# Loading a K cache in 8 KB rows and scoring four heads at once, in an attention decode kernel

## Chip, cores, metric

One core of a Trainium2 chip. The metric is device time in microseconds (us), lower is better. A program on one core has no other cores to be compared with, so a run counts as fast unless it is over 1.5% above the fastest of the same kernel; single looks have the state "unknown".

## The reference

```python
B, Sq, D = 32, 1, 512
Hq, Hkv, Sk, Dh = 32, 8, 2048, 128
W = 512                                   # the last 512 keys count
q = (x @ wq).reshape(B, 1, Hq, Dh)        # 4 query heads share one K/V head
k = k_cache[:, :, Sk - W:, :]             # per batch and head: 512 rows of 256 bytes, contiguous
v = v_cache[:, :, Sk - W:, :]
p = softmax(q @ k^T * Dh ** -0.5)
out = (p @ v) @ wo
```

All data is bf16. Of each batch the kernel reads 1 MB of K and 1 MB of V (8 heads x 512 keys x 256 bytes), for 32 batches; with wq and wo (4 MB each) that is 75.5 MB. Nothing is read twice. The window of one head is 128 KB long, and the next head's window begins 512 KB further on.

## The kernel before

SyncE (SP) issues all loads in one queue: K and V of each batch in turn, K into 4 slots, V into 12. For each batch TensorE transposes K in 32 pieces of 128 x 128 into PSUM (the memory that its results go to), VectorE copies three quarters of it back and ScalarE one quarter, and TensorE makes the scores: eight matmuls, one for each K/V head, of 32 weights columns and 512 moving columns. The weights (QBD) are zero except for the four query heads that belong to that K/V head, so eight accumulating matmuls fill 32 rows. Softmax, the transpose of P and the product with V are done for four batches (a quad) at a time.

```python
def load_k(b):                                    # on SP
    if b >= NK:
        sp.wait_ge(pe_T3, b - NK + 1)             # slot free: transposes of batch b-4 done
    sp.dma_start(
        K_sb[:, b % NK, :, :],
        k_cache[b, :, SK - W:, :].rearrange("g (p kt) d -> p g (kt d)", kt=KT),
    ).then_inc(sem_k[b % NK], 16)
# ...
for g in range(G):                                # scores, on TensorE
    # ... wait for the eviction of head g
    last = pe.matmul(
        S_ps[32 * j:32 * (j + 1), q % 2, :],      # j: batch in its quad
        lhsT=QBD[:, b % NQB, g, :],
        rhs=KT_sb[:, b % NKT, g, :],
        start=(g == 0), stop=(g == G - 1), tile_position=(0, 32 * j),
    )
```

The access pattern of the K load: partition p takes keys 4p to 4p+3 of each head, in memory 128 rows at an even pitch, each with 8 pieces (the heads) of 1 KB.

## Time and profile before

229.98 us, median of 3 runs (229.43 to 230.52). The page of the profile, cut; rows of digits are 40 equal slices of the span, 9 is busy to 90% or more:

```profile
span 228.2 us, 5628 instructions
PE 176.6 (77%) x2501; PEld 124.7 (55%) x2501; DVE 90.0 (39%) x237; ACT 48.1 (21%) x93; POOL 9.4 (4%) x43
...
DMA  6999999999999999999999999999999999999950
GB/s 188 386 385 348 348 348 349 348 348 350 349 347 348 349 347 348 348 348 348 348 348 348 347 348 348 348 348 348 347 347 348 347 348 347 349 345 329 350 183 6
DMA packets 72950, 75.90 MB, mean 333 GB/s; under 512 B 1184, under 2 KB 70880, under 8 KB 72928
...
DMA 53%; PE 26%; SPq 16%; issue 2%; DVEq 0%; DVE 0%; ACT 0%
...
L234 PE MATMUL KT_ps<-ident,K_sb 128*128 128x128 bf16 x1024 | 74.3, 240 | 29.7 <-DMA K_sb<-in_k_cache_dram 25.6
L254 PE MATMUL S_ps<-KT_sb,QBD 128*32 128x512 bf16 x256 | 68.2, 414 | 2.8 <-POOL QBD L191 2.8
...
K_sb<-in_k_cache_dram SPq DMA_DIRECT2D x32, 1024.0 KB, 12.1
V_sb<-in_v_cache_dram SPq DMA_DIRECT2D x24, 1024.0 KB, 12.0
```

The DMA row is full from the second slice until the last loads, and the rate stays near 348 GB/s while K and V are loaded; TensorE is busy 77% of the time and VectorE 39%. The loads bound the kernel. The second and third slices hold wq alone, and run at 386: wq comes in packets of 2 KB, K, V and wo in packets of 1 KB.

The same by stretches (columns: stretch and length in us, busy time and instructions of each engine, granted TensorE clock, DMA share, GB/s):

```profile
core 0: us, PE busy (x) PEld busy (x) DVE busy (x) ACT busy (x) POOL busy (x), PEclk, DMA share, GB/s
26.00:60.00 34.00, 26.35 (x350) 18.38 (x347) 13.84 (x39) 7.78 (x15) 1.05 (x5) 0.95 1.10 349
...
170.00:194.00 24.00, 21.81 (x289) 15.77 (x289) 9.17 (x26) 4.53 (x9) 0.00 (x0) 0.79 1.10 348
```

The rate is the same where TensorE's clock was 0.95 and where it was 0.79: compute does not set the pace.

### The profile page before, as it was taken

To read this page: it belongs to the slowest core of one execution; us is meant where nothing else is said; L and a number is where in the kernel's file an instruction comes from. 1 tells how busy PE (TensorE), PEld (TensorE's weight loads), DVE (VectorE), ACT (ScalarE), POOL (GpSimd) and SP (SyncE) were. 2 spreads that over 40 slices of the span, in tenths; PEclk is the share of its full clock that TensorE was granted. 3 is DMA by queue.
4 is the path that set the end of the run, shared out by engine and by line. 5 is a ranking of instruction groups with operands and counts; after the bars stand their busy time and mean duration, and the time that the engine had idled before them with its cause. 6 is when DMAs were issued, how large, how long until landed. Compare 5 with 4: busy or idle time off the path is not lost.

```text
span 228.2 us, 5628 instructions
## 1 busy us (share of the span) xinstructions
PE 176.6 (77%) x2501; PEld 124.7 (55%) x2501; DVE 90.0 (39%) x237; ACT 48.1 (21%) x93; POOL 9.4 (4%) x43
## 2 busy tenths in 40 slices
PE   0184968669869986995997996699669799999482
PEld 0182555447635753575564964477437656695340
DVE  0047333351535243633275243524353317644212
ACT  2000103122113211320133021321132013403203
POOL 5002000000000000000000000000000000000000
PEclk9998879999997999797699889889997859979855
DMA  6999999999999999999999999999999999999950
GB/s 188 386 385 348 348 348 349 348 348 350 349 347 348 349 347 348 348 348 348 348 348 348 347 348 348 348 348 348 347 347 348 347 348 347 349 345 329 350 183 6
DMA packets 72950, 75.90 MB, mean 333 GB/s; under 512 B 1184, under 2 KB 70880, under 8 KB 72928
## 3 DMA queue, kind: packets, MB, share of 16 engines
q1 hardware_dynamic: 72928, 75.57, 103.7%
q8 instruction: 19, 0.31, 0.6%
q14 instruction: 3, 0.02, 0.0%
HBM read 75.53 MB, written 0.03 MB: 331 GB/s over the span
## 4 chain that ended last, share of the span: by engine, by line
DMA 53%; PE 26%; SPq 16%; issue 2%; DVEq 0%; DVE 0%; ACT 0%
DMA K_sb<-in_k_cache_dram 48%; PE KT_ps L234 12%; PE S_ps L254 7%; PE QO_ps L286 6%; SPq L142 6%; DMA wo_sb<-in_wo_dram 5%; SPq L132 5%; SPq L149 4%; SPq L124 2%; PE PT_ps L266 1%; PE KT_ps L315 0%; DVEq L43 0%; DVE X_sb L389 0%; PE QO_ps L324 0%; ACT out_sb L441 0%
## 5 line engine op out<-in xcount | busy, mean ns | idle before, releaser
L234 PE MATMUL KT_ps<-ident,K_sb 128*128 128x128 bf16 x1024 | 74.3, 240 | 29.7 <-DMA K_sb<-in_k_cache_dram 25.6
L348 DVE COPY KT_sb<-KT_ps 128x512 bf16<-128x512 bf16 x192 | 68.0, 418 | 68.0 <-PE KT_ps L234 67.3
L234 PEld LDWEIGHTS KT_ps<-ident,K_sb 128*128 128x128 bf16 x1024 | 67.8, 108 | 42.1 <-DMA K_sb<-in_k_cache_dram 34.9
L254 PE MATMUL S_ps<-KT_sb,QBD 128*32 128x512 bf16 x256 | 68.2, 414 | 2.8 <-POOL QBD L191 2.8
L405 ACT ACTIVATE KT_sb<-KT_ps 128x512 bf16<-128x512 bf16 x64 | 34.7, 594 | 161.6 <-PE KT_ps L234 161.6
L254 PEld LDWEIGHTS S_ps<-KT_sb,QBD 128*32 128x32 bf16 x256 | 23.7, 102 | 34.8 <-issue 8.2
L286 PEld LDWEIGHTS QO_ps<-PT_sb,V_sb 128*128 128x128 bf16 x768 | 20.0, 97 | 3.2 <-ACT PT_sb L422 2.1
L286 PE MATMUL QO_ps<-PT_sb,V_sb 128*128 128x4 bf16 x768 | 20.7, 165 | 0.8 <-ACT PT_sb L422 0.7
L370 DVE CAST oT_sb<-QO_ps 128x128 bf16<-128x128 f32 x8 | 5.8, 719 | 38.8 <-PE QO_ps L286 38.8
L191 POOL COPY QBD<-QT_sb 128x32 bf16<-128x32 bf16 x32 | 6.3, 209 | 152.7 <-PE S_ps L254 135.8
L214 PE MATMUL QO_ps<-xT_sb,big_sb 128*128 128x32 bf16 x128 | 4.1, 185 | 8.4 <-DMA big_sb<-in_wq_dram 8.3
L336 DVE CAST QT_sb<-QO_ps 128x512 bf16<-128x512 f32 x2 | 4.8, 2393 | 13.0 <-PE QO_ps L214 13.0
L214 PEld LDWEIGHTS QO_ps<-xT_sb,big_sb 128*128 128x128 bf16 x128 | 3.8, 103 | 8.7 <-issue 6.7
L286 PEld LDWEIGHTS QO_ps<-PT_sb,big_sb 128*128 128x128 bf16 x256 | 6.5, 96 | 0.8 <-ACT PT_sb L422 0.8
L286 PE MATMUL QO_ps<-PT_sb,big_sb 128*128 128x4 bf16 x256 | 6.7, 164 | 0.0
L413 ACT ACTIVATE P_f_56<-S_ps,negmax 128x512 f32<-128x512 f32 x8 | 5.5, 687 | 4.0 <-DVE negmax L356 4.0
L354 DVE TENSOR_REDUCE maxv<-S_ps 128x1 f32<-128x512 f32 x8 | 5.5, 682 | 1.0 <-PE S_ps L254 1.0
L266 PE MATMUL PT_ps<-ident,P_bf 128*128 128x128 bf16 x32 | 3.6, 242 | 2.5 <-DVE P_bf L364 2.5
L422 ACT ACTIVATE PT_sb<-PT_ps 128x512 bf16<-128x512 bf16 x8 | 4.8, 604 | 1.2 <-PE PT_ps L266 1.2
L315 PE MATMUL KT_ps<-wo_sb,oT_sb 128*32 128x512 bf16 x32 | 3.9, 626 | 0.9 <-DVE oT_sb L370 0.8
L266 PEld LDWEIGHTS PT_ps<-ident,P_bf 128*128 128x128 bf16 x32 | 2.5, 111 | 3.0 <-DVE P_bf L364 3.0
L364 DVE TENSOR_SCALAR P_bf<-P_f_56,recip 128x512 bf16<-128x512 f32 x8 | 3.9, 486 | 0.3
(25 smaller groups left out, 14.7 us busy)
## 6 DMA issues: line engine op xcount, KB each, us to landing
K_sb<-in_k_cache_dram SPq DMA_DIRECT2D x32, 1024.0 KB, 12.1
V_sb<-in_v_cache_dram SPq DMA_DIRECT2D x24, 1024.0 KB, 12.0
big_sb<-in_v_cache_dram SPq DMA_DIRECT2D x8, 1024.0 KB, 12.0
big_sb<-in_wq_dram SPq DMA_DIRECT2D x4, 1024.0 KB, 10.8
wo_sb<-in_wo_dram SPq DMA_DIRECT2D x4, 1024.0 KB, 12.0
x_sb<-in_x_dram SPq DMA_DIRECT2D x1, 32.0 KB, 1.6
out_dram<-out_sb SPq DMA_DIRECT2D x1, 32.0 KB, 1.5
```

The costliest lines, as they stand in the source:

```text
L132: sp.dma_start(K_sb[:, b % NK, :, :], k_cache[b, :, SK - W:, :].rearrange("g (p kt) d -> p g (kt d)", kt=KT),).then_inc(sem_k[b % NK], 16)
L142: sp.dma_start(v_slot(b)[:, :, :], v_cache[b, :, SK - W:, :].rearrange("g (p kt) d -> p g (kt d)", kt=KT),).then_inc(sem_v[b % NV], 16)
L149: sp.dma_start(wo_sb[:, c * 8:(c + 1) * 8, :], wo[c * 1024:(c + 1) * 1024, :].rearrange("(h d) n -> d h n", d=P),).then_inc(sem_wo[c], 16)
L191: pool.tensor_copy(dst, src).then_inc(pool_qbd, 1)
L214: last = pe.matmul(QO_ps[:, hl * 32:(hl + 1) * 32], lhsT=wq_sb[:, kt, h * DH:(h + 1) * DH], rhs=xT_sb[:, kt, :], start=(kt == 0), stop=(kt ...
L234: last = pe.matmul(KT_ps[:, t, half * 512 + kt * 128: half * 512 + (kt + 1) * 128], lhsT=K_sb[:, b % NK, g, kt * DH:(kt + 1) * DH], rhs=id ...
L254: last = pe.matmul(S_ps[32 * j:32 * (j + 1), q % 2, :], lhsT=QBD[:, b % NQB, g, :], rhs=KT_sb[:, b % NKT, g, :], start=(g == 0), stop=(g = ...
L266: last = pe.matmul(PT_ps[:, kt * 128:(kt + 1) * 128], lhsT=P_bf[:, qq % 2, kt * 128:(kt + 1) * 128], rhs=ident[:, :], start=True, stop=Tru ...
L286: last = pe.matmul(QO_ps[:, j * 32 + 4 * g: j * 32 + 4 * g + 4], lhsT=v_slot(b)[:, g, kt * DH:(kt + 1) * DH], rhs=PT_sb[:, qq % 2, kt * 12 ...
L348: dve.tensor_copy(KT_sb[:, b % NKT, g, :], KT_ps[:, t, half * 512:(half + 1) * 512]).then_inc(dve_T, 1)
L370: dve.tensor_copy(oT_sb[:, :, 4 * qq:4 * qq + 4].rearrange("p h j -> p j h"), QO_ps[:, 0:128].rearrange("p (j h) -> p j h", h=HQ),).then_i ...
L405: act.activation(KT_sb[:, b % NKT, g, :], KT_ps[:, t, half * 512:(half + 1) * 512], ACTF.Copy).then_inc(act_T, 1)
```

## The change

Its intent: read K in rows of 8 KB, so that there are 128 large packets per batch instead of 1024 small ones, and let four score matmuls run at once on four column groups of TensorE's array (32 columns each, by `tile_position`). Partition p = 8 s + g now holds 32 keys in a row (the s-th of 16 groups) of head g. Transposing such a tile through a permutation matrix, not the identity, brings the keys of a head side by side. Score matmuls of heads g and g + 4 accumulate in the rows of column group g % 4; scores are made one batch later, and pairs of evictions become one. P is read in permuted order to match V.

```diff
-                    K_sb[:, b % NK, :, :],
-                    k_cache[b, :, SK - W:, :].rearrange("g (p kt) d -> p g (kt d)", kt=KT),
+                    K_sb[:, b % NK, :],
+                    k_cache[b, :, SK - W:, :].rearrange("g (s r) d -> s g (r d)", s=16),
 ...
+            pool.affine_select(
+                out=perm[:, :, :], in_=perm[:, :, :], compare_op=ALU.not_equal, fill=1.0,
+                base=0, pattern=[[-1, G], [-8, 16]], channel_multiplier=1,
 ...
+                    for i in range(8):
+                        r = 8 * t + i
+                        last = pe.matmul(
+                            KT_ps[:, t, i * 128:(i + 1) * 128],
+                            lhsT=K_sb[:, b % NK, r * DH:(r + 1) * DH],
+                            rhs=perm[:, :, :],
 ...
-                        S_ps[32 * j:32 * (j + 1), q % 2, :],
+                        S_ps[32 * (g % 4):32 * (g % 4) + 32, q % 2, :],
                         lhsT=QBD[:, b % NQB, g, :],
-                        rhs=KT_sb[:, b % NKT, g, :],
-                        start=(g == 0), stop=(g == G - 1), tile_position=(0, 32 * j),
+                        rhs=KT_sb[:, b % NKT, :, g, :],
+                        start=(j == 0 and g < 4), stop=(j == 3 and g >= 4), tile_position=(0, 32 * (g % 4)),
 ...
-                    for half in range(2):
-                        g = 2 * t + half
-                        dve.tensor_copy(
-                            KT_sb[:, b % NKT, g, :], KT_ps[:, t, half * 512:(half + 1) * 512]
-                        ).then_inc(dve_T, 1)
+                    dve.tensor_copy(
+                        KT_sb[:, b % NKT, 8 * t:8 * t + 8, :, :], KT_ps[:, t, :]
+                    ).then_inc(dve_T, 1)
 ...
-                    P_bf[:, qq % 2, :], P_f32[:, qq % 2, :], recip[:, qq:qq + 1], None, op0=ALU.mult
+                    P_bf[:, qq % 2, :].rearrange("p (kt s u) -> p kt s u", kt=KT, s=16),
+                    P_f32[:, qq % 2, :].rearrange("p (u kt s) -> p kt s u", kt=KT, s=16),
+                    recip[:, qq:qq + 1], None, op0=ALU.mult,
```

The K load of the changed kernel reads 16 groups (8 KB apart) of 8 rows (512 KB apart) of 4096 elements and writes 128 partitions; before it read 128 groups of 8 pieces of 512 elements.

More of the change, by code (lines that the diff above doesn't have):

```diff
@@ L47, in bass_standalone__sliding_block_cached__sampling_kernel @@
         wo_sb = es.enter_context(nc.sbuf_tensor([P, HQ, D], BF16))
-        K_sb = es.enter_context(nc.sbuf_tensor([P, NK, G, KT * DH], BF16))
+        K_sb = es.enter_context(nc.sbuf_tensor([P, NK, 32 * DH], BF16))
         V_sb = es.enter_context(nc.sbuf_tensor([P, NVA, G, KT * DH], BF16))
-        KT_sb = es.enter_context(nc.sbuf_tensor([P, NKT, G, W], BF16))
+        KT_sb = es.enter_context(nc.sbuf_tensor([P, NKT, 32, G, 16], BF16))
         QT_sb = es.enter_context(nc.sbuf_tensor([P, B, HQ], BF16))
@@ L58, in bass_standalone__sliding_block_cached__sampling_kernel @@
         ident = es.enter_context(nc.sbuf_tensor([P, P], BF16))
+        perm = es.enter_context(nc.sbuf_tensor([P, G, 16], BF16))
         X_sb = es.enter_context(nc.sbuf_tensor([P, D], BF16))
@@ L91, in bass_standalone__sliding_block_cached__sampling_kernel @@
         pool_R = es.enter_context(nc.semaphore("pool_R"))
+        pool_perm = es.enter_context(nc.semaphore("pool_perm"))
         dve_xT = es.enter_context(nc.semaphore("dve_xT"))
@@ L113, in v_slot, with prow @@
             return Vx_sb[:, s - NVA]
+        def prow(g, j):
+            return 32 * (g % 4) + 16 * (g // 4) + 4 * j
         def quad_of(b):
@@ L172, in _ @@
             ).then_inc(pool_init, 1)
+            pool.memset(perm[:, :, :], 0.0).then_inc(pool_perm, 1)
+            pool.wait_ge(pool_perm, 1)
+            pool.affine_select(
+                out=perm[:, :, :], in_=perm[:, :, :], compare_op=ALU.not_equal, fill=1.0,
+                base=0, pattern=[[-1, G], [-8, 16]], channel_multiplier=1,
+            ).then_inc(pool_perm, 1)
             pool.memset(QBD[:, :, :, :], 0.0).then_inc(pool_init, 1)
@@ L188, in _ @@
                 n = b % NQB
-                dst = bass.AP(tensor=QBD, offset=n * G * 32, ap=[[qbd_row, P], [36, G], [1, REP]])
-                src = bass.AP(tensor=QT_sb, offset=b * HQ, ap=[[qt_row, P], [REP, G], [1, REP]])
+                dst = bass.AP(
+                    tensor=QBD, offset=n * G * 32 + 4 * (b % 4),
+                    ap=[[qbd_row, P], [144, 2], [32, 4], [1, REP]],
+                )
+                src = bass.AP(
+                    tensor=QT_sb, offset=b * HQ, ap=[[qt_row, P], [4 * REP, 2], [REP, 4], [1, REP]]
+                )
                 pool.tensor_copy(dst, src).then_inc(pool_qbd, 1)
@@ L222, in transposes @@
             def transposes(b):
+                if b == 0:
+                    pe.wait_ge(pool_perm, 2)
                 pe.wait_ge(sem_k[b % NK], 16 * (b // NK + 1))
@@ L226, in transposes @@
                         if t < 3:
-                            pe.wait_ge(dve_T, 6 * (b - 1) + 2 * (t + 1))
+                            pe.wait_ge(dve_T, 3 * (b - 1) + t + 1)
                         else:
-                            pe.wait_ge(act_T, 2 * b)
+                            pe.wait_ge(act_T, b)
                     last = None
-                    for half in range(2):
-                        g = 2 * t + half
-                        for kt in range(KT):
-                            last = pe.matmul(
-                                KT_ps[:, t, half * 512 + kt * 128: half * 512 + (kt + 1) * 128],
-                                lhsT=K_sb[:, b % NK, g, kt * DH:(kt + 1) * DH],
-                                rhs=ident[:, :],
-                                start=True, stop=True, is_transpose=True, tile_position=(0, 0),
-                            )
+                    for i in range(8):
[4 more added lines that the diff above has]
+                            rhs=perm[:, :, :],
+                            start=True, stop=True, is_transpose=True, tile_position=(0, 0),
+                        )
                     last.then_inc(pe_T[t], 1)
@@ L248, in s_matmuls @@
                 last = None
+                pe.wait_ge(dve_T, 3 * b + 3)
+                pe.wait_ge(act_T, b + 1)
                 for g in range(G):
-                    if g < 6:
-                        pe.wait_ge(dve_T, 6 * b + g + 1)
-                    else:
-                        pe.wait_ge(act_T, 2 * b + (g - 6) + 1)
                     last = pe.matmul(
-                        S_ps[32 * j:32 * (j + 1), q % 2, :],
+                        S_ps[32 * (g % 4):32 * (g % 4) + 32, q % 2, :],
                         lhsT=QBD[:, b % NQB, g, :],
-                        rhs=KT_sb[:, b % NKT, g, :],
-                        start=(g == 0), stop=(g == G - 1), tile_position=(0, 32 * j),
+                        rhs=KT_sb[:, b % NKT, :, g, :],
+                        start=(j == 0 and g < 4), stop=(j == 3 and g >= 4), tile_position=(0, 32 * (g % 4)),
                     )
@@ L288, in pv_matmuls @@
                                 lhsT=v_slot(b)[:, g, kt * DH:(kt + 1) * DH],
-                                rhs=PT_sb[:, qq % 2, kt * 128 + j * 32 + 4 * g: kt * 128 + j * 32 + 4 * g + 4],
+                                rhs=PT_sb[:, qq % 2, kt * 128 + prow(g, j): kt * 128 + prow(g, j) + 4],
                                 start=(kt == 0), stop=(kt == KT - 1), tile_position=(0, 0),
@@ L297, in _ @@
             qt_pass(1)
-            s_matmuls(0)
             for b in range(1, B):
@@ L303, in _ @@
                     pt_transposes(q - 1)
-                s_matmuls(b)
+                s_matmuls(b - 1)
                 if j == 1 and q >= 1:
                     pv_matmuls(q - 1)
+            s_matmuls(B - 1)
             pt_transposes(NQUAD - 1)
@@ L345, in kt_evacs @@
                     dve.wait_ge(pe_T[t], b + 1)
-                    for half in range(2):
-                        g = 2 * t + half
-                        dve.tensor_copy(
-                            KT_sb[:, b % NKT, g, :], KT_ps[:, t, half * 512:(half + 1) * 512]
-                        ).then_inc(dve_T, 1)
+                    dve.tensor_copy(
+                        KT_sb[:, b % NKT, 8 * t:8 * t + 8, :, :], KT_ps[:, t, :]
+                    ).then_inc(dve_T, 1)
             def softmax_a(qq):
@@ L402, in kt_evacs @@
                     act.wait_ge(pe_T[t], b + 1)
-                    for half in range(2):
-                        g = 2 * t + half
-                        act.activation(
-                            KT_sb[:, b % NKT, g, :], KT_ps[:, t, half * 512:(half + 1) * 512], ACTF.Copy
-                        ).then_inc(act_T, 1)
+                    act.activation(
+                        KT_sb[:, b % NKT, 8 * t:8 * t + 8, :, :], KT_ps[:, t, :], ACTF.Copy
+                    ).then_inc(act_T, 1)
             def do_exp(qq):
```

## The prediction

> **What bounds the kernel now.** The stream of loads. In the page's 40 slices DMA is full (9) from the second slice to the last but two, at 345 to 350 GB/s wherever K, V and wo are loaded; 75.5 MB are read. PE is busy 77%, DVE 39%. The windows view gives 348 GB/s also where PE's granted clock was 0.79. The loads wait for PE to free K slots (39.8 us in 19 pieces, waits of the DMA queue), but this never empties the stream: about four loads are in flight (12.1 us to landing, 3 us each). The chain of waits ends in the last wo load (222.5 us), then a tail of 5.7 us.
>
> **Why 348.** Packet size. Slices 2 and 3 hold wq alone, in 2 KB packets: 386 GB/s. K, V and wo come in 1 KB packets: 348. Over 16 engines that is 84.9 and 47.1 ns a packet: 37.8 ns per KB and 9.3 ns per packet.[...]
>
> **What the change does.**
> - K (33.6 MB) comes in 8 KB rows: estimate 9.3 + 8 x 37.8 = 312 ns, 420 GB/s. K's share falls from 96.4 to about 80 us: 16 us off the critical path. V and wo stay.
> - Score matmuls on four column groups at once. Now 8 take 1.83 us at full clock. The wo product already runs so: four 512-column matmuls per 0.43 us at half clock. So 8 should take 0.45 to 0.9 us, saving 35 to 40 us of PE time, none of it on the path.
> - Evictions: pairs of 128x512 (DVE 0.35 us each back to back, ACT 0.54) become one 128x1024: estimate 0.63 and 1.05 us. Hidden.
> - P scaled with a permuted read: 0.49 us may become 0.6 to 0.8; hidden behind wo. Scores move one batch later; POOL's extra memset and select hide behind the first loads.
>
> **Does anything else become the bound?** A batch's loads fall from 6.0 to 5.5 us. PE needs about 2.0 (transposes) + 0.5 + 0.9 (PV, PT) = 3.4 us at full clock, about 5.5 at half clock throughout. Four K slots keep several loads queued, so short stalls don't empty the stream. After the last K load, V and wo still take 15 us; the compute behind it took 11.7, so it stays hidden, with 3 us to spare.
>
> **Predicted: 214.5 us**, 80% range 210.5 to 219.5. Chances: faster by over 2% 0.88, within 2% 0.06, slower 0.06.
>
> **What would show each step.** Rate about 380 GB/s where K and V alternate (wo still 348); packets down by about 28,700; score matmuls' stretch a third or less; PE below 65% busy; DMA full in every slice to the end; the chain still ends wo load, wo product, output, tail 5.7 us. If K's rate is right but the time isn't, gaps in the DMA row would show it, with the queue waiting on transposes.
>
> **What would make it wrong.** (1) The K load's source now has 16 x 8 rows against 128 partitions; if that spreads badly over the 16 engines, K could be slower than 348, and the kernel 240 us or more. (2) The packet cost isn't linear beyond 2 KB, or rows are cut: 4 KB packets would give 408 GB/s and 215.7 us. (3) [...]the last batch's compute overruns the wo loads: 1 to 5 us. (4) Score matmuls reading 32-byte pieces run far slower than contiguous ones.

Two passages are cut from it: a remark on the cost of a packet and the reason given for doubt (3); the 1 to 5 us there is my estimate. The sum: the measured 230 us less about 16 us of K, put at 214.5 us. The eviction times of 0.63 and 1.05 us and the 0.6 to 0.8 us for P are estimates as well, from the 0.35, 0.54 and 0.49 us of the trace; all are called hidden, so the sum does not use them.

## The result, and the profile after

334.29 us, median of 4 runs (329.5 to 338.86), against 229.83: slower, by a ratio of 1.4394 (95% interval 1.4324 to 1.4464). Ratios here are the mean time of one kernel's fast runs over that of the other's in the same rounds, so they are not quite the ratio of the medians quoted. Two of the changed kernel's four runs (336.8 and 338.86) lie over 1.5% above its fastest and count as slow; the ratio rests on the two fast ones, 329.5 and 331.78, with a mean of 330.6, and comparisons below use that. The profile is of the 329.5 us run.

The page of the changed kernel, the lines that answer to those above:

```profile
span 327.4 us, 5510 instructions
PE 175.5 (54%) x2501; PEld 143.0 (44%) x2501; DVE 91.4 (28%) x141; ACT 46.2 (14%) x61; POOL 9.9 (3%) x45
...
DMA  6999999999999999999999999999999999999960
GB/s 155 382 321 264 233 231 214 246 248 253 241 238 244 244 230 232 230 227 223 229 226 212 224 216 217 230 221 232 224 230 225 236 238 228 236 237 229 301 220 4
DMA packets 44277, 75.90 MB, mean 232 GB/s; under 512 B 1184, under 2 KB 38112, under 8 KB 40160
...
DMA 64%; SPq 22%; PE 11%; DVE 1%; issue 1%; ACT 1%; DVEq 0%; ACTq 0%
...
L251 PE MATMUL KT_ps<-perm,K_sb 128*128 128x128 bf16 x1024 | 112.0, 307 | 125.2 <-DMA K_sb<-in_k_cache_dram 120.5
L269 PE MATMUL S_ps<-KT_sb,QBD 128*32 128x512 bf16 x256 | 26.8, 508 | 0.3 <-ACT KT_sb L418 0.3
...
K_sb<-in_k_cache_dram SPq DMA_DIRECT2D x32, 1024.0 KB, 23.6
V_sb<-in_v_cache_dram SPq DMA_DIRECT2D x24, 1024.0 KB, 20.9
```

The DMA row looks the same as before: full. But full at 230 GB/s, not 348. Below 8 KB there are now 40,160 packets of 44,277; the other 4,117 include K's 4,096 rows, so the 8 KB rows are there, uncut. The wq load in the second slice still runs at 382; the rate falls as soon as K loads are in the mix. TensorE waits for K 120.5 us where it waited 25.6. Score matmuls did become cheap (68.2 to 26.8 us busy), and nobody gains from it.

By stretches, in the same columns:

```profile
26.00:100.00 74.00, 37.22 (x452) 30.42 (x452) 19.63 (x30) 9.45 (x11) 1.67 (x8) 0.65 1.04 243
100.00:180.00 80.00, 47.21 (x628) 38.59 (x628) 24.41 (x41) 12.67 (x18) 1.67 (x8) 0.66 1.06 228
```

The granted clock is 0.65 where it was 0.95 to 0.79. That is why the transposes' busy time rose from 74.3 to 112.0 us with the same count: by the trace's records of the clock, one transpose took about 62 ns of busy time at full clock and about 111 at half, in both kernels, and 182 of the 1,024 fell wholly into half clock before, 928 in the changed kernel. Why less clock was granted is not shown: in kpool below TensorE is busy for less of the span (47% against 54%), and its mean clock is higher (0.73 against 0.68). The slower transposes do not set the time: TensorE is busy 50% and 59% of these stretches (37.22 of 74 us, 47.21 of 80) and waits for K in the rest.

The trace also records each DMA packet with its size and time. Sorted by size (my count from these records; 1 KB packets are V, wo and, before, K):

```
kernel    size    count    median ns   mean ns
before    1 KB    69,696     51          51.5
changed   1 KB    36,928     75          75.1
changed   8 KB     4,096    567.5       562.0
```

I had estimated 312 ns for 8 KB. They take 562, and the 1 KB packets of V, whose load was not touched, also slowed by half.

### The profile page after: what moved, and what is told of

Read it like the earlier page. It is cut to its first block, busy times and chain, and to the rows that moved or that the text cites. A ratio compares the mean times of both kernels' runs of the same rounds, so it can differ in the third digit from the quotient of the medians.

```text
span 327.4 us, 5510 instructions
## 1 busy us (share of the span) xinstructions
PE 175.5 (54%) x2501; PEld 143.0 (44%) x2501; DVE 91.4 (28%) x141; ACT 46.2 (14%) x61; POOL 9.9 (3%) x45
## 2 busy tenths in 40 slices
DMA packets 44277, 75.90 MB, mean 232 GB/s; under 512 B 1184, under 2 KB 38112, under 8 KB 40160
## 4 chain that ended last, share of the span: by engine, by line
DMA 64%; SPq 22%; PE 11%; DVE 1%; issue 1%; ACT 1%; DVEq 0%; ACTq 0%
DMA K_sb<-in_k_cache_dram 64%; SPq L137 16%; PE KT_ps L251 8%; SPq L147 4%; SPq L129 1%; PE KT_ps L330 1%; PE QO_ps L301 1%; ACT KT_sb L418 0%; DVEq L43 0%; DVE oT_sb L385 0%; DVE maxv L367 0%; DVE X_sb L404 0%; PE S_ps L269 0%; DVE P_bf L377 0%; PE QO_ps L339 0%
## 5 line engine op out<-in xcount | busy, mean ns | idle before, releaser
L251 PE MATMUL KT_ps<-perm,K_sb 128*128 128x128 bf16 x1024 | 112.0, 307 | 125.2 <-DMA K_sb<-in_k_cache_dram 120.5
L251 PEld LDWEIGHTS KT_ps<-perm,K_sb 128*128 128x128 bf16 x1024 | 104.0, 145 | 142.1 <-DMA K_sb<-in_k_cache_dram 137.1
L361 DVE COPY KT_sb<-KT_ps 128x1024 bf16<-128x1024 bf16 x96 | 66.4, 693 | 152.7 <-PE KT_ps L251 150.2
L418 ACT ACTIVATE KT_sb<-KT_ps 128x1024 bf16<-128x1024 bf16 x32 | 32.7, 1023 | 259.6 <-PE KT_ps L251 259.6
L269 PE MATMUL S_ps<-KT_sb,QBD 128*32 128x512 bf16 x256 | 26.8, 508 | 0.3 <-ACT KT_sb L418 0.3
L269 PEld LDWEIGHTS S_ps<-KT_sb,QBD 128*32 128x32 bf16 x256 | 4.3, 104 | 6.6 <-issue 5.8
L426 ACT ACTIVATE P_f<-S_ps,negmax 128x512 f32<-128x512 f32 x8 | 5.5, 687 | 6.6 <-DVE negmax L369 6.6
L281 PE MATMUL PT_ps<-ident,P_bf 128*128 128x128 bf16 x32 | 4.4, 281 | 2.7 <-DVE P_bf L377 2.7
L377 DVE TENSOR_SCALAR P_bf<-P_f,recip 128x512 bf16<-128x512 f32 x8 | 5.2, 651 | 0.3
```

What stands on the lines that cost most here:

```text
L251: last = pe.matmul(KT_ps[:, t, i * 128:(i + 1) * 128], lhsT=K_sb[:, b % NK, r * DH:(r + 1) * DH], rhs=perm[:, :, :], start=True, stop=True ...
L269: last = pe.matmul(S_ps[32 * (g % 4):32 * (g % 4) + 32, q % 2, :], lhsT=QBD[:, b % NQB, g, :], rhs=KT_sb[:, b % NKT, :, g, :], start=(j == ...
L281: last = pe.matmul(PT_ps[:, kt * 128:(kt + 1) * 128], lhsT=P_bf[:, qq % 2, kt * 128:(kt + 1) * 128], rhs=ident[:, :], start=True, stop=Tru ...
L361: dve.tensor_copy(KT_sb[:, b % NKT, 8 * t:8 * t + 8, :, :], KT_ps[:, t, :]).then_inc(dve_T, 1)
L418: act.activation(KT_sb[:, b % NKT, 8 * t:8 * t + 8, :, :], KT_ps[:, t, :], ACTF.Copy).then_inc(act_T, 1)
```

## Experiments

Eleven kernels, named by their labels. The diffs are cut to the lines that matter, against the changed kernel where nothing else is said. How rows are dealt to the DMA engines is a supposition. A warning on the word "correct" first: the scores of these inputs are at most 0.0006 in size, so softmax is flat and the comparison with the reference passes whatever K is. I therefore also ran the kernels' values through a simulator off the chip with wq 4000 times larger (scores up to 2.4). Against an fp32 calculation the relative rms error was 0.0034 for the kernels before and changed and for rows32x4, kpool8x4, kpool, colgroups, sp8x4 and rows16x8_1k, and 0.63 for flat128, as it should be.

**flat128: an even pitch.**

```diff
-                    k_cache[b, :, SK - W:, :].rearrange("g (s r) d -> s g (r d)", s=16),
+                    bass.AP(tensor=k_cache.tensor, offset=k_cache.offset + b * HKV * SK * DH,
+                            ap=[[2 * 4096, 128], [1, 4096]]),
```

> Wrong result on purpose. The changed kernel, but each K load reads 128 rows of 8 KB at one even pitch of 16 KB (other addresses, same bytes and packets), so the source has 128 rows against 128 partitions, not 16 x 8. Theory A (the 16 x 8 shape[...]): 8 KB packets near 312 ns, some 380 GB/s, 212 to 218 us. Rival B (8 KB packets are slow as such, or beside 1 KB ones): unchanged, 325 to 340 us, 8 KB packets near 565 ns. Rival C (the 512 KB pitch between heads makes HBM slow): as fast as A says.

**near16x8: the shape without the far pitch.**

```diff
+                            ap=[[9 * 4096, 16], [4096, 8], [1, 4096]]),
```

> Wrong result on purpose. The changed kernel, but each K load reads 16 groups of 8 adjoining rows of 8 KB, groups 72 KB apart: the shape 16 x 8 as in the change, without the 512 KB pitch between heads. A: still slow, 320 to 340 us, 8 KB packets near 565 ns. B: still slow. C: fast, 212 to 218 us.

**flat128far: the far pitch without the shape.**

```diff
+    offset=k_cache.offset + (b % 2) * 16 * HKV * SK * DH + (SK - W) * DH + (b // 2) * 4096,
+    ap=[[SK * DH, 128], [1, 4096]]
```

> Wrong result on purpose. The changed kernel, but each K load reads 128 rows of 8 KB, one from each (batch, head), at an even pitch of 512 KB. A: fast, 212 to 218 us. B: slow, 325 to 340 us. C: slow, 300 us or more, as every row now lies 512 KB from the next.

Measured, one look each: flat128 214.15 us, near16x8 327.84, flat128far 214.44 (before, on the same chip: 229.52). The stretches of flat128 and then of near16x8, in the columns of above:

```profile
26.00:100.00 74.00, 53.26 (x911) 43.77 (x910) 31.88 (x54) 17.10 (x22) 2.73 (x13) 0.80 1.06 381
100.00:180.00 80.00, 61.76 (x994) 49.77 (x993) 37.74 (x64) 19.93 (x26) 2.30 (x11) 0.76 1.06 381
```

```profile
60.00:260.00 200.00, 121.15 (x1698) 100.66 (x1699) 61.30 (x98) 30.11 (x40) 4.40 (x21) 0.65 1.06 234
```

The DMA share is 1.06 in both; the rate is 381 and 234. The 8 KB packets took a median of 314 ns in flat128 and in flat128far, and 567 in near16x8. So 8 KB packets are not slow as such (B falls), nor does a 512 KB pitch slow these loads (C falls). The one property that the two slow kernels share, and the two quick ones lack, is the 16 x 8 shape of the source against 128 partitions.

flat128 differs from the changed kernel in the source of the K load alone (its addresses, and with them its shape), and so gives the size of it. The span is 327.4 - 212.4 = 115 us shorter. Over 16 engines the packets account for that: (562 - 324) ns x 4,096 / 16 = 61 us from the 8 KB packets, and (75.1 - 50.3) ns x 36,928 / 16 = 57 us from the 1 KB packets beside them (means; 324 and 50.3 are flat128's).

**rows16x8_1k: the shape, with small packets.**

```diff
+                for c in range(8):
+                    sp.dma_start(
+                        K_sb[:, b % NK, 512 * c:512 * (c + 1)],
+                        k_cache[b, :, SK - W:, :].rearrange("g (s r) d -> s g (r d)", s=16)[:, :, 512 * c:512 * (c + 1)],
+                    ).then_inc(sem_k[b % NK], 16)
```

> Right result. The changed kernel with each K load cut into eight of 16 x 8 rows of 1 KB: the change's shape, the packets of the kernel before. A (shape alone costs, whatever the packet): 1 KB packets of K clearly slower than 51 ns, 270 us or more. If only 8 KB packets suffer from the shape: 229 to 233 us.

302.52 us (one look), 73 us over the kernel before, whose packets are as large. The stretch in the middle:

```profile
60.00:260.00 200.00, 123.82 (x1752) 102.93 (x1752) 64.39 (x104) 32.66 (x43) 4.18 (x20) 0.65 0.97 254
```

So the loss is not peculiar to 8 KB packets, but how much of the 73 us is the shape's is not shown. The trace does not tell K's 1 KB packets from V's; of both together the median stayed at 51 ns, and the mean rose from 51.5 to 61.2, which over 69,696 packets and 16 engines is 42 us. The rest goes with a DMA share of 0.97 where the kernel before has 1.10: each batch has eight K loads here and not one, and no run tests eight loads with an even pitch. At 8 KB the shape costs 116 us (330.6 against flat128's 214.15). The even pitch gives 229.8 us at 1 KB and 214.15 at 8 KB, so the packet size itself gained what it was meant to gain.

**half_0_63 and half_32_95: the same load to other partitions.** From the fifth batch on both load only heads 0 to 3, 16 x 4 rows (the first four loads are those of flat128). They differ in the destination alone; the diff is of one against the other. The sharp form of theory A was that the destination counts too: partitions 0 to 63 slow, 32 to 95 quick.

```diff
-                        K_sb[0:64, b % NK, :],
+                        K_sb[32:96, b % NK, :],
                         k_cache[b, 0:4, SK - W:, :].rearrange("g (s r) d -> s g (r d)", s=16),
```

> Wrong result on purpose: from the fifth batch on only half of K is loaded, 16 x 4 rows of 8 KB (the change's rows of heads 0 to 3), to partitions 0 to 63. Theory A in its sharp form[...]: 8 KB packets near 565 ns, 210 us or more. If the shape of the source (16 groups) is what slows a load whatever it is written to: the same here, and the same in half_32_95.

> Wrong result on purpose: the same loads as in half_0_63, same source, same shape 16 x 4, but to partitions 32 to 95[...]. A in its sharp form: 8 KB packets near 312 to 325 ns, 178 to 190 us. If the shape of the source is what slows: as slow as half_0_63.

Measured (one look each): 233.96 and 180.24 us. Stretches of half_0_63, then of half_32_95:

```profile
60.00:180.00 120.00, 83.69 (x1282) 68.39 (x1279) 48.26 (x80) 25.79 (x34) 3.78 (x18) 0.73 1.04 254
```

```profile
60.00:140.00 80.00, 70.47 (x1370) 58.97 (x1371) 45.52 (x79) 24.04 (x33) 3.36 (x16) 0.85 1.07 370
```

Source, shape, packet size and queue are equal, and the rate is 254 in one and 370 in the other; the 8 KB packets' median is 492 ns and 316 (without the first 512 packets, of the four full loads in the good shape, 562 and 316). So with the source held fixed, addresses and all, it is where the data is written that decides.

What is shown is this: with the same destination the shape of the source sets the rate (381 GB/s in flat128, 234 in near16x8), and with the same source the destination does (254 and 370 in this pair). Why these pairs of source and destination are slow is not shown: the trace does not name the engine of a packet, so which engine wrote where is not known.

**kpool: the same loads from POOL.**

```diff
-                sp.dma_start(
+                pool.dma_start(
                     K_sb[:, b % NK, :],
                     k_cache[b, :, SK - W:, :].rearrange("g (s r) d -> s g (r d)", s=16),
```

> Right result. The changed kernel with its K loads (same shape, same addresses, same packets) issued from POOL[...], not from SP. A[...]: 8 KB packets near 312 ns, 212 to 219 us, faster than the kernel before. A, if it spreads them as SP's does, and B and C: 320 us or more.

290.8 us (4 runs, ratio 1.2671, 1.2625 to 1.2716). POOL issues each K load between its own copies. Its K loads are in a queue of their own, `q0 software_dynamic` in its page (33.56 MB, beside 42.01 MB in `q1 hardware_dynamic`), but that did not cure it: the 8 KB packets' median was 576 ns. It is still 12% quicker than the changed kernel (290.8 / 330.6); K and V are in two queues here, and its rate alternates between slices near 230 and slices near 345 GB/s.

```profile
GB/s 201 248 234 233 374 349 266 228 230 229 243 343 222 227 223 348 286 229 226 295 327 227 229 258 348 260 229 229 287 311 238 241 271 344 233 256 346 343 290 9
```

I had put this branch ("spreads them as SP's does") at 320 or more. The packets say where the difference lies: K's are as slow as in the changed kernel (mean 568 ns against 562), but the 1 KB packets took a mean of 56.8 ns and not 75.1, which is (75.1 - 56.8) ns x 36,928 / 16 = 42 us, against a difference of 40 us in the times.

**colgroups: the compute half alone, on the kernel before.**

```diff
-                        S_ps[32 * j:32 * (j + 1), q % 2, :],
+                        S_ps[32 * (g % 4):32 * (g % 4) + 32, q % 2, :],
 ...
+                        start=(j == 0 and g < 4), stop=(j == 3 and g >= 4), tile_position=(0, 32 * (g % 4)),
```

> Right result. The kernel before with the compute half of the change alone: score matmuls of four heads on four column groups; K in 1 KB rows, as before. Theory (the loads bound the kernel, the shape of the K load alone made the change slow): 228 to 231 us, same as before; score matmuls' busy time 68 us falls to 20 to 30. Rival D (the new score matmuls[...] cost time): over 235 us.

229.27 us, ratio 0.9974 (0.9946 to 1.0002): the same. The compute half neither helps nor hurts where the loads bind. Its busy time was a miss:

```profile
L262 PE MATMUL S_ps<-KT_sb,QBD 128*32 128x512 bf16 x256 | 52.9, 453 | 3.8 <-POOL QBD L199 2.8
```

52.9 us, not 20 to 30. Here each matmul still waits for its own head's eviction, as before, so four may rarely start together; in the change all these waits stand ahead of the eight matmuls. No run tests whether that is the reason.

**rows32x4: a repair on SP.** Two loads per batch of four heads each, 32 groups of 4 rows of 4 KB. The permutation, the score operand and the order of P follow.

```diff
+                for h in range(2):
+                    sp.dma_start(
+                        K_sb[:, b % NK, h * 2048:(h + 1) * 2048],
+                        k_cache[b, 4 * h:4 * h + 4, SK - W:, :].rearrange("g (s r) d -> s g (r d)", s=32),
+                    ).then_inc(sem_k[b % NK], 16)
 ...
-                base=0, pattern=[[-1, G], [-8, 16]], channel_multiplier=1,
+                base=0, pattern=[[-1, 4], [-4, 32]], channel_multiplier=1,
 ...
-                        rhs=KT_sb[:, b % NKT, :, g, :],
+                        rhs=KT_sb[:, b % NKT, 16 * (g // 4):16 * (g // 4) + 16, g % 4, :],
```

> Right result. The changed kernel with each K load in two, of four heads each: 32 x 4 rows of 4 KB to 128 partitions, issued from SP. If only an even pitch over 128 rows is spread well[...]: slow, 300 us or more. If groups of four partitions are enough: 4 KB packets near 161 ns, 214 to 219 us.

216.74 us, ratio 0.9427 (0.94 to 0.9454), right result: 5.7% faster than the kernel before. The 4 KB packets' median was 164 ns. With 32 groups of four rows the load is quick (376 GB/s, in the stretch below); an even pitch over 128 rows is not needed. By which rule rows are dealt to the engines is not shown.

**kpool8x4: a repair on POOL, with 8 KB rows.** Four loads per batch, of 8 groups x 4 rows to 32 partitions each.

```diff
+                for sh in range(2):
+                    for gh in range(2):
+                        p0, k0 = 64 * gh + 32 * sh, SK - W + 256 * sh
+                        pool.dma_start(
+                            K_sb[p0:p0 + 32, b % NK, :],
+                            k_cache[b, 4 * gh:4 * gh + 4, k0:k0 + 256, :].rearrange("g (s r) d -> s g (r d)", s=8),
+                        ).then_inc(sem_k[b % NK], 16)
```

> Right result. K loads issued from POOL, each in four of 8 x 4 rows of 8 KB to 32 partitions[...]. A: 8 KB packets near 312 to 325 ns, 212 to 222 us. If all four loads fall to the same eight engines[...]: 260 us or more.

215.44 us, ratio 0.9374 (0.9342 to 0.9406), right result: 6.3% faster than the kernel before, and within 1.3 us of flat128. The 8 KB packets' median was 316 ns. Stretches of kpool8x4 and of rows32x4:

```profile
60.00:180.00 120.00, 80.22 (x1512) 65.74 (x1508) 53.22 (x94) 30.76 (x40) 46.30 (x98) 0.77 1.06 376
```

```profile
60.00:180.00 120.00, 88.74 (x1544) 73.23 (x1540) 55.94 (x93) 29.34 (x39) 3.98 (x19) 0.81 1.06 376
```

**sp8x4: the same four loads, from SP.**

```diff
-                        pool.dma_start(
+                        sp.dma_start(
```

> Right result. The same K loads of 8 x 4 rows as in kpool8x4, but issued from SP. If SP gives a load of eight groups always to the same eight engines[...], these eight carry all of K, 4.2 MB each at 26.3 GB/s beside their share of the rest: 8 KB packets stay near 312 to 325 ns, but the time goes to 270 to 300 us. If SP spreads them over 16 engines[...]: 213 to 218 us.

335.02 us (one look). It is slow, as in the first branch, and slower than the 270 to 300 that I gave it. The profile:

```profile
DMA  4996777777788787886778887778887967669860
...
q1 hardware_dynamic: 44768, 75.57, 76.3%
```

This DMA row is far from full: packets take 76% of the 16 engines' time, where they took 101% in the changed kernel (`q1` in its page). That fits the first branch, in which eight engines carry all of K, but does not prove it. The small packets differ as well: the page of the changed kernel counts 1,184 under 512 B, 16 for each of its 74 DMA issues, and that of sp8x4 1,696; with 16 for each of the other 42 issues, 8 are left for each of its 128 K loads. For the same loads from POOL kpool8x4's page leaves 48 (6,816 less 672, over 128). What they stand for, and which engines carried K, the trace does not say. What is shown is the time: the same four loads took 335.02 us from SP and 215.44 from POOL. Part of the missed size is that the packets, put at 312 to 325 ns, did not keep that time: the 8 KB ones took a mean of 384 ns (median 316) and the 1 KB ones 61.7, so some were slowed here as well; why was not taken apart.

## Why the prediction was wrong

- **The step that failed** is "K (33.6 MB) comes in 8 KB rows: estimate 9.3 + 8 x 37.8 = 312 ns, 420 GB/s", together with "V and wo stay". It took the rate of a load to depend on its packet size alone. In the shape 16 x 8 the packets took 562 ns, and those of V went from 51 to 75. Two terms of the sum were mis-sized, by 61 and 57 us.
- **The estimate of the packet itself was right, for a load with an even pitch.** In flat128 the 8 KB packets took a median of 314 ns, the stretch ran at 381 GB/s where I had said 380, and the time was 214.15 us where I had said 214.5 (closer than the end of the kernel deserved: see the chain of waits below).
- **The shape that cost the time stood in the prediction as doubt (1)**, with 240 us or more, and I gave slower only 0.06. (That the load is spread badly over the engines, as it says, was not shown.) What I knew then should have made me weigh it more: the built load has 16 outer groups against 128, no load of the kernel before has that shape, and the fit to its packets could not speak for it.
- **What bounds the kernel, and that compute is hidden: right, but for the end.** The loads still bound it (DMA row full, TensorE waiting for K), and colgroups moved nothing.
- **The sizes of compute: mostly right.** Eight score matmuls, reading 32-byte pieces, took 0.62 us at full clock and about 1.0 at the lower one (said: 0.45 to 0.9); evictions 0.69 and 1.02 us (0.63 and 1.05); P scaled 0.65 (0.6 to 0.8); packets fell by 28,673 (28,700). In busy time the score matmuls fell to 0.39 of before (26.8 of 68.2 us), where I had said a third or less. TensorE is below 65% busy (54%), as said, but because the span grew.
- **The check "DMA full in every slice" held and was worthless**: a slowed packet counts as busy for as long as it takes (a DMA share of 1.06 at 381 GB/s in flat128 and at 228 in the changed kernel). The rate beside it told the truth.
- **The chain of waits** was to end in the wo load, with compute 3 us ahead. In the changed kernel it ends in the last K load and the compute behind it, the wo product included; K loads are 64% of the span in it, where they were 48%. In flat128, whose loads ran as predicted, it ends in compute too: the last packet of wo was done 7.1 us before the end, and 6.2 us in the kernel before, so the overrun of doubt (3) cost about 1 us (an estimate from these two).

What stays open: what slows the packets in this shape, to 1.73 times the 324 ns of flat128 (562 / 324), and why the 1 KB packets beside them slow as well (50.3 to 75.1 ns). The trace does not say which engine a packet is from.

## What to carry to other kernels

When a load is reshaped for larger packets, look at the built access patterns on both sides, not only at the bytes in a row: here an outer dimension of 16 against 128 partitions cost 116 us, while 32 x 4 rows of 4 KB (216.74 us), or an even pitch over 128 (214.15), came out near the predicted 214.5. A full DMA row says that packets are in flight, not that they are quick (a DMA share of 1.06 here at 381 GB/s and at 228), so read GB/s and the time of one packet beside it. And when a change couples a memory layout to a compute improvement, run the layout alone with any data: one look at such a load would have shown the loss.
